# Attention and a rational MLP on one core: the local scores of a batch's first four heads in one burst on TensorE

## The chip, the cores and the metric

The kernel runs on one core of a Trainium2 chip. A core has TensorE (PE, with its weight loads shown apart as PEld), VectorE (DVE), ScalarE (ACT), GpSimd (POOL) and SyncE (SP); each works through its own list of instructions in order and waits on semaphores for the others. SP and POOL also issue DMA transfers. The time is device microseconds (us) of one execution, as the median of three runs.

## The reference

The input is q, k and v of 8 batches, 8 heads, 576 rows and 64 columns, and the weights and six coefficients of an MLP. All is float32.

```
q_d, k_d, v_d = mean over 4 neighbouring rows of q, k, v       # 144 rows
pooled = softmax(q_d k_d^T / 8) v_d, each row repeated 4 times
local  = softmax(q k^T / 8 where |i - j| < 4, else -1e9) v     # a band
x = (pooled + local), heads side by side                        # 4608 x 512
h = x @ w_in                                                    # 4608 x 2048
g = (a0 + a1 h + a2 h^2 + a3 h^3) / (1 + |b0||h| + |b1| h^2 + 1e-6)
out = g @ w_out                                                 # 4608 x 512
```

## The kernel before

**MLP.** Most of TensorE's time goes to the two products. A step takes a block of tokens through one piece of the 2048 columns. `h_part` multiplies into one of two PSUM banks, 2 and 3, which the steps use in turn: in fp32 from the decoded weights `wb` for the first 16 steps (L1546, four matmuls a step), and later from `xs` with the weights split in two fp32r parts `wh` and `wl` (L1560). ACT reads the bank four times with polynomials of h (`act`, L1574, into `m`, `n`, `gb`, `line`), DVE combines them (`rational`, L1603 to L1619, into `g` or `gg`), and `o_part` (L1639) multiplies with the second weights into banks 4 to 7. A bank of h can be written again when its four readers on ACT are done. In the first fifth of the run ACT and DVE also decode and split the weights (`sl` L573, `wb` L579, `wh` L596, `wl` L598).

**Attention.** It runs beside this, a batch ahead, with banks 0 and 1 for its scores. A `Half` is four heads of a batch in two pairs (`self.cs`). The band is computed on ten windows of 58 keys. For a half TensorE has three bursts of small matmuls between the big ones: `scores` (L999, 20 matmuls: the local scores of the first pair), `scores_rest` (L1041 and L1052, 32 matmuls: the local scores of the second pair and the pooled scores of both) and `weight_both` (L884 and L1372, 52 matmuls: the weighting with v). A batch has six such bursts from batch 3 on. What doesn't fit in banks 0 and 1 is lent from the two h banks for a moment (`Loan`): the next step that would use that bank waits for the DVE mask that empties it (L1082). DVE adds the mask to each pair's scores as it takes them from PSUM (L1009, L1082, L1091), then takes the row maximum (L1111), and ACT the exponentials (L1122). To turn the weights round, DVE transposes in blocks and SP sends the blocks out and back: four DMA issues `fd<-fx` for each pair (L1272), four `fp<-epb` for each half's pooled part (L1299).

In the small matmuls, two row tiles (the upper and lower 64 partitions) may write one bank. Where they do, `passed` and `behind` let PE signal SP and SP signal back, so that the second waits for the first. In `scores_rest` eight small matmuls stand between the two lines, and in `weight_both` many more; `scores` has no such hop.

```
                before = passed(local(3, 0))
...
                behind(local(0, 1), before)
```

**Order.** A `Plan` writes every engine's list before the kernel is built. Pieces are added with an engine, an estimated duration, what they read and write, and a due time; the plan lays them out by due times, pushes pieces that came late, and tries this 400 times from a fixed seed. Due times come from the constants at the file's end (`H_FIRST` and `H_STEP` for the MLP steps, `SCORES_EARLY`, `DUES`, `LEADS` for the bursts of a half, `KEEPDUE`, `FETCH`, `AHEAD`, `LATE` for weights, loads and so on). So one change in a piece or a constant moves pieces all over the program.

Of the kernel before, what the change touches and what calls it, by code (L numbers as in the profile page):

```python
# [15 lines left out]
ALU = mybir.AluOpType  # L16
# [5 lines left out]
P = 128  # L22
# [14 lines left out]
NW = 10  # L37
# [58 lines left out]
    )  # L96


class Plan:


# [70 lines left out]
    def run(self):  # L172


        kept = [(t, dict(t.preds), list(t.succs), t.lag) for t in self.tasks]

        def again():
            for t, preds, succs, lag in kept:
                t.preds, t.succs, t.lag, t.start = dict(preds), list(succs), lag, None
            return self.once()  # L180

        dice = random.Random(SEED)
        best, bias = None, [0.0] * len(kept)
        for n in range(PASSES):
            for t, x in zip(self.tasks, bias):
                t.bias = x
            if n:
                self.push(dice)
            tried = [t.bias for t in self.tasks]
            again()  # L190
# [30 lines left out]
    def once(self):  # L221
# [21 lines left out]
        while len(done) < len(self.tasks):  # L243
# [44 lines left out]
            if t.loan is not None:  # L288
                t.loan.room = self.turns[n][0]
                users = [x for x in t.succs if x.engine != "PE"]  # L290
                users = [x for x in users if t.loan.keys & x.takes]
                self.lent.setdefault(n, []).extend(users)
                if n + 2 in self.turns:
                    h = self.turns[n + 2][1][0]
                    for q in (open_["PE"], waiting["PE"]):
                        if any(x[2] is h for x in q):
                            q[:] = [x for x in q if x[2] is not h]
                            heapq.heapify(q)
                    todo = []
                    for x in users:  # L300
                        h.preds[x] = False
                        x.succs.append(h)
                        left[h] += 1
                        todo.append((x, h))
                    while todo:
                        x, y = todo.pop()
                        late = y.late - x.dur - self.gap(x, y)
# [19 lines left out]
def attention_moe(  # L327
# [631 lines left out]
    class Half:  # L959
# [64 lines left out]
                )  # L1024
            self.softmax(c)

        def scores_rest(self, bk):

            o = self.cs[1]
            n4 = NQ * SD  # L1030
            bc = Loan()

# [26 lines left out]
            def issue():  # L1059
# [14 lines left out]
                local(4, 0)  # L1074

            add(
                "PE", SREST, issue, (o.slot.qk, *(c.means for c in self.cs)), (*bk, bc),
                due=self.due - self.lead - SCORES_EARLY[1]
            ).step = ROOM[0]
            def masked():  # L1080
                n4_ = 4 * QD
                nc.vector.tensor_tensor(  # L1082
                    out=o.slot.eq.ap.rearrange("p b (j c) k -> p j b (c k)", j=2)[:, ::-1, :, :n4_],
                    in0=bc.ap.rearrange("p (j b n) -> p j b n", j=2, b=2),
                    in1=maskd.ap.rearrange("p b c k -> p b (c k)")[:, :, :n4_].unsqueeze(1).broadcast_to([P, 2, 2, n4_]),
                    op=ALU.add,
# [2 lines left out]
            def masked_last(g):  # L1089
                gs = slice(g * D, (g + 1) * D)  # L1090
                nc.vector.tensor_tensor(  # L1091
                    out=o.slot.eq.ap.rearrange("p b (j c) k -> p j c b k", j=2)[gs, :: 2 * g - 1, 4],
                    in0=two(bk)[gs, :, n4 : n4 + D].rearrange("p j (b k) -> p j b k", b=2),
                    in1=maskd.ap[gs, :, 4].unsqueeze(1).broadcast_to([D, 2, 2, QD]), op=ALU.add
                )
# [662 lines left out]
    for w, f, spot in chunks[len(early) :]:  # L1758
        weights(w, f, spot)

    def attend(b):

        if b == PFLIP:
            own = pools[0]
            pads = own.eb.ap.rearrange("p h b i k c -> p (h b i k) c")[:, :, QB:]
            add("POOL", 0.5, lambda: nc.gpsimd.memset(pads, 0.0), (), (own.e, *own.rooms))
        early, gap = (SPLIT_EARLY, QUAD_GAP) if b < LATER else ENDS
        last = due_h(blocks[b].first) - early - 3.0
# [38 lines left out]

    begun = []

    def begin_half(b, q):  # L1810
        early, gap = (SPLIT_EARLY, QUAD_GAP) if b < LATER else ENDS
        last = due_h(blocks[b].first) - early - 3.0
        bk = banks[0:2]
        k = 2 * (b - LATER) + q
        half_ = Half(b, q, last - (1 - q) * gap + (DUES[k] if k >= 0 else 0.0))
        half_.lead = LEADS[k] if k >= 0 else 0.0
        half_.load()
        c = half_.cs[0]
        if b in PEMASK:
            scores(c, bk)  # L1820
# [82 lines left out]
PAIRS = (14, 128)  # L1903
KEPT = 2
UNIT0 = 0
KEEPDUE = 307.365
FETCH = -15.499
O_LAG = 4.049
H0 = 20.57
H_FIRST = 5.91  # L1910
H_STEP = 5.979
SPLIT_EARLY = 5.529
QUAD_GAP = 42.0
LATER = 2
ENDS = (11.53, 52.06)
SCORES_EARLY = (38.82, 49.09)
WARM = 0.6
EP_DVE = (1, 3)
LEAD = 13.84
# [2 lines left out]
BOTH = 1  # L1922
SOON = 1.2
SPOTS = (0, 1, 2, 3, 6, 0, 1, 4, 5, 2, 3)
LATE = 0.083
MINUS = (0, 1, 2, 3)
POOLED = (2, 3)
VBANK = (0, 0)
POOLDUE = 0.0
FILL = 17  # L1930
KEEP = 3
AHEAD = 14.6
# [8 lines left out]
DUES = (-5.76, -9.77, -3.13, -7.81, -2.8, -4.74, -2.31, -2.62, -4.58, -8.38, -2.54, -4.74)  # L1941
LEADS = (0.17, 10.7, 5.25, -3.78, -8.15, -0.78, 0.3, -0.47, 2.8, 3.6, -2.67, -0.87)
AHEAD_S = 1
FLIPLAG = (3.4, 5.0, 4.5, 6.5)
FLIPSP = 2.0
# [80 lines left out]
```

## Time and profile before

| what | value |
|---|---|
| median of 3 runs | 919.04 us (918.35 to 919.2) |
| the profiled execution, its own time | 918.93 us |
| span of its records | 917.2 us |
| PE busy | 905.3 us, 99% |
| DVE busy | 836.4 us, 91% |
| ACT busy | 749.0 us, 82% |
| granted TensorE clock, mean | 0.999 |

The profiled execution is 0.11 us below the median, and 1.73 us of it lie around the span. PE has almost no idle time, but a busy PE isn't the same as a PE at its pace: records of matmuls overlap, so the pace is read from the distance between starts (a 128x512 matmul's record lasts 0.39 us, and the next one starts 0.23 us after it). Each float32 matmul on small tiles leaves two records, so a burst of 20 matmuls shows as x40.

### The profile page before, as it was taken

To read this page: it belongs to the slowest core of one execution; us is meant where nothing else is said; L and a number is where in the kernel's file an instruction comes from. 1 tells how busy PE (TensorE), PEld (TensorE's weight loads), DVE (VectorE), ACT (ScalarE), POOL (GpSimd) and SP (SyncE) were. 2 spreads that over 40 slices of the span, in tenths; PEclk is the share of its full clock that TensorE was granted. 3 is DMA by queue.
4 is the path that set the end of the run, shared out by engine and by line. 5 is a ranking of instruction groups with operands and counts; after the bars stand their busy time and mean duration, and the time that the engine had idled before them with its cause. 6 is when DMAs were issued, how large, how long until landed. Compare 5 with 4: busy or idle time off the path is not lost.

```text
span 917.2 us, 18534 instructions
## 1 busy us (share of the span) xinstructions
PE 905.3 (99%) x7039; PEld 718.6 (78%) x7039; DVE 836.4 (91%) x1004; ACT 749.0 (82%) x1738; POOL 171.9 (19%) x237
## 2 busy tenths in 40 slices
PE   8999999999999999999999999999999999999998
PEld 6655667888888888888888888888888888888886
DVE  8899999999998999989998999999899888788984
ACT  5899999978887879788897888787979776677853
POOL 3222022122311213031403131222210100110010
PEclk9999999999999999999999999999999999999999
DMA  9988888758894869687878778586944340224033
GB/s 317 333 241 254 254 218 233 205 127 216 185 302 129 210 181 215 222 176 223 200 248 182 243 181 264 141 248 183 262 121 132 134 137 1 92 92 138 1 115 114
DMA packets 85370, 171.28 MB, mean 187 GB/s; under 512 B 10914, under 2 KB 50338, under 8 KB 85282
## 3 DMA queue, kind: packets, MB, share of 16 engines
q0 software_dynamic: 32224, 72.30, 33.8%
q1 hardware_dynamic: 52914, 97.68, 31.7%
q8 instruction: 55, 0.90, 0.4%
q14 instruction: 33, 0.27, 0.1%
q10 hardware_dynamic: 144, 0.13, 0.1%
HBM read 140.58 MB, written 29.49 MB: 185 GB/s over the span
## 4 chain that ended last, share of the span: by engine, by line
PE 90%; ACT 7%; DVE 2%; issue 1%; DMA 1%; SPq 0%; DVEq 0%
PE psum L1639 41%; PE psum L1560 38%; PE psum L1546 3%; ACT m L1574 2%; PE psum L884 2%; ACT gb L1574 1%; PE psum L1372 1%; ACT el L775 1%; PE psum L1041 1%; PE psum L999 1%; PE psum L1052 1%; DMA qk<-in_qk_dram 1%; ACT wh L596 1%; ACT epc L806 1%; ACT sl L573 0%
## 5 line engine op out<-in xcount | busy, mean ns | idle before, releaser
L1639 PE MATMUL psum<-wh,gg 128*128 128x512 f32 x912 | 297.4, 393 | 0.0
L1560 PE MATMUL psum<-xs,wh 128*128 128x512 f32 x1024 | 256.4, 390 | 0.0
L1560 PEld LDWEIGHTS psum<-xs,wh 128*128 128x128 f32 x1024 | 191.3, 188 | 41.4 <-ACT n L1574 1.3
L1639 PEld LDWEIGHTS psum<-wh,gg 128*128 128x128 f32 x912 | 169.3, 188 | 36.2 <-DVE gg L1619 0.2
L1639 PE MATMUL psum<-wl,gg 128*128 128x512 f32 x456 | 177.6, 389 | 0.0
L1574 ACT ACTIVATE m<-psum,cf 128x512 f32<-128x512 f32 x172 | 128.4, 755 | 40.8 <-PE psum L1560 35.0
L1560 PE MATMUL psum<-xs,wl 128*128 128x512 f32 x512 | 137.1, 390 | 0.0
L1574 ACT ACTIVATE n<-psum,cf 128x512 f32<-128x512 f32 x116 | 86.3, 752 | 53.6 <-PE psum L1560 48.9
L1560 PEld LDWEIGHTS psum<-xs,wl 128*128 128x128 f32 x512 | 96.0, 188 | 20.0
L1639 PEld LDWEIGHTS psum<-wl,gg 128*128 128x128 f32 x456 | 85.6, 188 | 17.8
L1574 ACT ACTIVATE line<-psum,cf 128x512 f32<-128x512 f32 x114 | 91.1, 800 | 0.4 <-DVE m L1607 0.4
L656 POOL DMA_DIRECT2D vpc<-in_vp_dram x42 | 36.6, 872 | 242.8 <-DMA vpc<-in_vp_dram 231.6
L443 POOL DMA_DIRECT2D wl<-ws x48 | 31.3, 651 | 263.0 <-PE psum L1639 259.6
L1603 DVE SCALAR_TENSOR_TENSOR m<-m,cf,m 128x512 f32<-128x512 f32 (+1 forms) x58 | 58.1, 1002 | 18.2 <-ACT m L1574 18.0
L656 POOL DMA_DIRECT2D pqb<-in_qkb_dram x60 | 56.8, 995 | 81.2 <-DMA pqb<-in_qkb_dram 72.1
L1122 ACT ACTIVATE eq<-eq,nmb 128x64 f32<-128x64 f32 x200 | 66.8, 343 | 2.4 <-DVE nmb L1116 2.4
L1546 PE MATMUL psum<-xf,wb 128*128 128x512 f32 x128 | 59.6, 602 | 2.5 <-ACT gb L1574 1.6
L1639 PE MATMUL psum<-wh,g 128*128 128x512 f32 x160 | 56.8, 420 | 0.6 <-DVE g L1619 0.6
L1618 DVE TENSOR_TENSOR m<-m,m 128x512 f32<-128x512 f32 (+1 forms) x58 | 54.8, 945 | 1.0
L1606 DVE TENSOR_TENSOR m<-m,m 128x512 f32<-128x512 f32 (+1 forms) x58 | 54.5, 940 | 0.1
L1574 ACT ACTIVATE m<-psum 128x512 f32<-128x512 f32 x86 | 53.5, 623 | 0.5 <-PE psum L1560 0.5
L1603 DVE SCALAR_TENSOR_TENSOR n<-n,cf,n 128x1024 f32<-128x1024 f32 x29 | 37.1, 1279 | 13.3 <-ACT n L1574 13.2
(152 smaller groups left out, 1637.6 us busy)
## 6 DMA issues: line engine op xcount, KB each, us to landing
wh<-ws POOLq DMA_DIRECT2D x48, 512.0 KB, 5.4
wl<-ws POOLq DMA_DIRECT2D x48, 512.0 KB, 4.5
qk<-in_qk_dram SPq DMA_DIRECT2D x32, 590.0 KB, 6.3
vw<-in_vw_dram SPq DMA_DIRECT2D x32, 320.0 KB, 4.3
pqb<-in_qkb_dram POOLq DMA_DIRECT2D x60, 168.0 KB, 5.0
out_dram<-lv SPq DMA_DIRECT2D x32, 256.0 KB, 6.3
fd<-fx SPq DMA_DIRECT2D x96, 80.0 KB, 3.8
ef<-fd SPq DMA_DIRECT2D x24, 320.0 KB, 4.6
```

The lines of the kernel that those rows point to most:

```text
L443: "POOL", 1.0, lambda d=scratch[i][j], x=x: nc.gpsimd.dma_start(out=x.ap.bitcast(F32), in_=d),
L596: add("ACT", 0.88, lambda: nc.scalar.copy(out=hi.ap, in_=exact), (lo,), (hi,), due=due)
L656: lambda d=dst, x=x: nc.gpsimd.dma_start(out=d.ap, in_=x, accum_op=ALU.add),
L884: mms.append(nc.tensor.matmul(x.ap[j * D : (j + 1) * D, o : o + D].rearrange("p (a q) -> p a q", a=2), lhsT=c.slot.vw.ap[m : m + D, w, :], ...
L1122: nc.scalar.activation(out=e[:, n], in_=e[:, n], func=AF.Exp, bias=nm[:, n : n + 1], scale=scale, accum_out=sm[:, n : n + 1],)
L1546: nc.tensor.matmul(ph.ap, lhsT=bits2[0][fc // 2].ap[:, fc % 2, c, :].bitcast(F32), rhs=x.ap[:, c, :], start=(c == 0), stop=(c == NCC - 1),)
L1560: nc.tensor.matmul(ph.ap[:, f * t : (f + 1) * t], lhsT=(high, low)[j][0][fc].ap[:, c, :], rhs=blk.x[i].ap[:, c, :] if blk.b is not None el ...
L1574: return add("ACT", cost, lambda: nc.scalar.activation(out=to, in_=in_, func=func, **kw), (room_in, cf, *more), (out_,))
L1603: lambda: v.scalar_tensor_tensor(out=tb_, in0=tq_, scalar=b1, in1=tb_, op0=ALU.mult, op1=ALU.add),
L1606: dve(0.61, lambda: v.tensor_tensor(out=ta_, in0=ta_, in1=tq_, op=ALU.mult), (ta, tq), (ta,))
L1618: dve(0.61, lambda: v.tensor_tensor(out=tb_, in0=ta_, in1=tb_, op=ALU.subtract), (ta, tb), (tb,))
L1639: nc.tensor.matmul(ob[sub].ap, lhsT=g[i].ap[:, f0 : f0 + P], rhs=weight_out(k, fc, j).ap, start=(fc == 0 and m == 0), stop=(fc == NFC - 1 ...
```

## The change

From batch 3 on (`LENT[0]` is 3 before and after) a batch is written by a new function `attend_five`. The first half's `scores` gives way to `scores_two`, which issues the local scores of both pairs of that half, 40 matmuls, as one piece: 4 of the second pair's, then 20 of the first pair's, then 16 of the second pair's, the last 4 of them behind a hop over SP. Its output lies in banks 0 and 1 and in one lent bank, and three masks on DVE take it out. `scores_rest` then has the pooled scores of its own half and the local scores of one pair of the second half: the first half's call takes the second half's first pair, the second half's call its second pair. So a batch has bursts of 40, 32, 52, 32 and 52 matmuls, where it had 20, 32, 52, 20, 32 and 52. `weight_both` isn't changed. Beside this, many of the plan's constants have new values, and the plan goes on when a push leads it into a circle (`Stuck`).

```
+        def scores_two(self, bk):
+            a, o = self.cs
+            bc = Loan()
+            na, nb = NW // 2 * D, 3 * D
...
+            def issue():
+                mms = [one(o, k, j, j) for k in (3, 4) for j in range(2)]
+                before = passed(mms[2:])
+                for k in range(5):
+                    for j in range(2):
+                        for g in range(2):
+                            one(a, k, j, g)
+                for k in range(3):
+                    for j in range(2):
+                        for g in range(2):
+                            one(o, k, j, g)
+                behind([one(o, k, j, 1 - j) for k in (3, 4) for j in range(2)][:2], before)
+
+            add(
+                "PE", STWO, issue, (a.slot.qk, o.slot.qk), (*bk, bc, a.slot.el, o.slot.el), due=self.due - self.lead - SCORES_EARLY[0]
+            ).step = ROOM[0]
...
+            mask(a, lambda: both(0, na), 0, 5, bk, 0.74, 5)
+            mask(o, lambda: both(na, na + nb), 0, 3, bk, 0.47, 3)
+            mask(
+                o, lambda: bc.ap[:, : 4 * D].rearrange("p (j b n) -> p j b n", j=2, b=2), 3, 5, (bc,), 0.34, 2
+            )
+            self.softmax(a)
+            self.softmax(o)
+
+        def scores_rest(self, bk, o=None):
 
-            o = self.cs[1]
+            o = o or self.cs[1]
...
+    def attend_five(b):
+        bk = banks[0:2]
+        first = begun.pop()
+        first.load_rest()
+        second = make_half(b, 1)
+        second.load_one(0)
+        halves = first, second
+        for q, half_ in enumerate(halves):
+            invert(slots[0].sm, NW)
+            normalize(half_.cs[0], "local")
+            half_.flip(half_.cs[0])
+            if q:
+                half_.load_rest()
+            half_.scores_rest(bk, halves[1].cs[q])
+            half_.pooled(bk)
+            if q == 0:
+                second.load_one(1)
+                second.load_means()
+            elif b + 1 < B:
+                begun.append(begin_half(b + 1, 0))
+            half_.weight_both(bk)
+            if q and begun:
+                begun[0].load_rest()
...
+        if b >= LENT[0]:
+            half_.scores_two(bk)
+            return half_
...
-H_FIRST = 5.91
-H_STEP = 5.979
+H_FIRST = 5.786
+H_STEP = 5.967
...
-SCORES_EARLY = (38.82, 49.09)
+SCORES_EARLY = (-9.36, 48.83)
...
-SREST, ABOTH = 1.7, 2.2
-ROOM = (-0.63, 2.29, -4.75)
+SREST, ABOTH, STWO = 1.7, 2.2, 1.55
+ROOM = (-21.83, -2.37, -3.51)
...
```

Three places show what the new order is. The first is PE at the scores of a later batch's first heads; `qk0` and `qk1` are the loaded queries and keys of the two pairs, `xs` with `wh0`/`wl0` an h product, `gg` with `wh1`/`wl1` an o product. Before:

```order
L1560 MATMUL psum<-xs0_0_104,wl0_10_66 128x512 x4
L1639 MATMUL psum<-wh1_14_103,gg3_133 128x512 x4
L999 MATMUL psum<-qk0_156 64x2x32 x20
L1560 MATMUL psum<-xs0_0_104,wh0_12_94 128x512 x4
L1560 MATMUL psum<-xs0_1_105,wh0_12_94 128x512 x4
L1639 MATMUL psum<-wh1_12_102,gg0_130 128x512
```

After (L1724 is `o_part`, L1061 the merged burst):

```order
L1724 MATMUL psum<-wh1_14_103,gg2_132 128x512
L1724 MATMUL psum<-wl1_14_86,gg2_132 128x512
L1724 MATMUL psum<-wh1_14_103,gg3_133 128x512 x4
L1061 MATMUL psum<-qk1_162 64x2x32 x4
L1061 MATMUL psum<-qk0_156 64x2x32 x20
L1061 MATMUL psum<-qk1_162 64x2x32 x16
L1724 MATMUL psum<-wh1_12_102,gg0_130 128x512
```

The 20 matmuls have become 40 in one place between big matmuls, and an o product, not an h product, now follows them.

The second place is ACT at about 72 to 77 us, in the first fifth of the run; `m`, `gb` are the readers of an h bank, `et` and `eptc` copies for attention, `sl3` a weight's scales. Before:

```order
L596 CAST wh1_4_98<-wb1_4_77 128x1024
L1574 ACTIVATE m0_116<-psum,cf_146 128x512
L1574 ACTIVATE gb0_126<-psum,cf_146 128x512
L1574 ACTIVATE m1_117<-psum,cf_146 128x512
L1574 ACTIVATE m2_118<-psum 128x512
L848 ACTIVATE epc0_153<-epc0_153,smb0_150 128x3x48 x6
L1232 COPY et0_160<-psum 128x4x122
L1232 COPY et1_167<-psum 128x4x122
L1574 ACTIVATE m0_116<-psum,cf_146 128x512
L1574 ACTIVATE m1_117<-psum,cf_146 128x512
L1574 ACTIVATE m2_118<-psum 128x512
L1574 ACTIVATE gb2_128<-m1_117,cf_146 128x512
```

Next in that list stand `sl3`, a copy `eptc`, and then the fourth reader, `gb1<-psum`. After, from the same `gb0` on (L1659 is `act`):

```order
L1659 ACTIVATE gb0_126<-psum,cf_146 128x512
L1659 ACTIVATE m1_117<-psum,cf_146 128x512
L1659 ACTIVATE m2_118<-psum 128x512
L1659 ACTIVATE m0_116<-psum,cf_146 128x512
L860 ACTIVATE epc0_153<-epc0_153,smb0_150 128x3x48 x6
L1659 ACTIVATE gb1_127<-psum,cf_146 128x512
L1659 ACTIVATE m1_117<-psum,cf_146 128x512
L1659 ACTIVATE m2_118<-psum 128x512
L1659 ACTIVATE gb2_128<-m1_117,cf_146 128x512
L1317 COPY et0_160<-psum 128x4x122
L1317 COPY et1_167<-psum 128x4x122
```

The cast, both `et` copies, `gb2<-m1`, `sl3` and a copy `eptc` have moved from before the step's last reader of its h bank to behind it.

The third place is PE at the same time, around the product that waits for that bank. Before:

```order
L1546 MATMUL psum<-xf0_1_107,wb0_6_63 128x512 x4
L1190 MATMUL psum<-ident_141,epc0_153 112x112 x8
L1639 MATMUL psum<-wh1_2_97,g1_123 128x512
L1639 MATMUL psum<-wl1_2_74,g1_123 128x512
L1639 MATMUL psum<-wh1_2_97,g3_125 128x512 x4
L1546 MATMUL psum<-xf0_1_107,wb0_6_63 128x512 x2
```

After (L1631 is the fp32 h product, L1269 and L1275 transposes):

```order
L1631 MATMUL psum<-xf0_1_107,wb0_6_63 128x512 x3
L1269 MATMUL psum<-ident_141,el0_159 128x122 x4
L1269 MATMUL psum<-ident_141,el1_166 128x122 x4
L1631 MATMUL psum<-xf0_1_107,wb0_6_63 128x512 x3
L1275 MATMUL psum<-ident_141,epc0_153 112x112 x8
L1631 MATMUL psum<-xf0_1_107,wb0_6_63 128x512 x2
L1724 MATMUL psum<-wh1_2_97,g3_125 128x512 x4
```

The four o matmuls with `g3` and the eight transposes of `epc` stood ahead of the waiting product's matmuls and now stand among or behind them.

## Rows read from the trace of the kernel before

**Rows 1.** The page's head, and busy time by engine.
```profile
span 917.2 us, 18534 instructions
PE 905.3 (99%) x7039; PEld 718.6 (78%) x7039; DVE 836.4 (91%) x1004; ACT 749.0 (82%) x1738; POOL 171.9 (19%) x237
```

**Rows 2.** Waits of PE: what waited, for whom; us in total, times, longest.
```profile
PE psum L1546 <- ACT gb L1574: 1.6, 2, 1.3
```

**Rows 3.** Windows: us, busy (x count) by engine, PEclk, DMA share, GB/s.
```profile
60.00:80.00 20.00, 18.11 (x71) 11.03 (x69) 19.54 (x31) 19.97 (x46) 5.44 (x6) 1.00 0.89 272
300.00:500.00 200.00, 200.00 (x1628) 164.45 (x1628) 187.61 (x212) 169.45 (x428) 47.34 (x64) 1.00 0.78 207
```

**Rows 4.** Timeline of PE at a burst: start, duration, what; last, that line's group.
```profile
360.83 1.98 PE L1560 MATMUL psum<-xs,wh 128*128 128x512 f32 x8
362.65 1.07 PE L1560 MATMUL psum<-xs,wl 128*128 128x512 f32 x4
363.64 0.81 PE L999 MATMUL psum<-qk 64*64 64x64 f32 x40
364.39 2.12 PE L1560 MATMUL psum<-xs,wh 128*128 128x512 f32 x8
...
L999 PE MATMUL psum<-qk 64*64 64x64 f32 x400 | 8.1, 223 | 0.0
```

**Rows 5.** Timeline of PE where it waits; in brackets the idle time and its releaser.
```profile
65.88 0.39 PE L1639 MATMUL psum<-wl,g 128*128 128x512 f32 x1
66.86 1.39 PE L1639 MATMUL psum<-wh,g 128*128 128x512 f32 x5 [0.59 <-DVE g L1619]
...
73.56 0.93 PE L1190 MATMUL psum<-ident,epc 112*112 112x112 f32 x8
...
74.80 1.09 PE L1639 MATMUL psum<-wh,g 128*128 128x512 f32 x4
77.19 1.55 PE L1546 MATMUL psum<-xf,wb 128*128 128x512 f32 x3 [1.30 <-ACT gb L1574]
...
101.34 3.70 PE L1546 MATMUL psum<-xf,wb 128*128 128x512 f32 x8 [0.32 <-ACT gb L1574]
```

**Rows 6.** Timeline of ACT ahead of the wait at 77.19 us.
```profile
66.53 1.03 ACT L596 CAST wh<-wb 128x1024 fp32r<-128x1024 f32 x1
...
71.69 1.02 ACT L1232 COPY et<-psum 128x488 f32<-128x488 f32 x2
...
74.31 0.76 ACT L1574 ACTIVATE gb<-m,cf 128x512 f32<-128x512 f32 x1
74.92 1.18 ACT L573 ACTIVATE sl<-sl 128x1024 f32<-128x1024 f32 x1
75.96 0.50 ACT L1232 COPY eptc<-psum 112x384 f32<-112x384 f32 x1
76.32 0.83 ACT L1574 ACTIVATE gb<-psum,cf 128x512 f32<-128x512 f32 x1
```

**Rows 7.** Groups of DVE by shape: busy us, mean ns, idle before.
```profile
L1603 DVE SCALAR_TENSOR_TENSOR n<-n,cf,n 128x1024 f32<-128x1024 f32 x29 | 37.1, 1279 | 13.3 <-ACT n L1574 13.2
L1009 DVE TENSOR_TENSOR eq<-psum,maskd 128x640 f32<-128x640 f32 x10 | 8.2, 815 | 0.7 <-PE psum L999 0.7
L1082 DVE TENSOR_TENSOR eq<-psum,maskd 128x512 f32<-128x512 f32 x10 | 6.9, 686 | 1.6 <-PE psum L1041 1.6
```

**Rows 8.** Timelines of DVE and PE after a `scores_rest` burst.
```profile
486.44 0.69 DVE L1082 TENSOR_TENSOR eq<-psum,maskd 128x512 f32<-128x512 f32 x1 [1.26 <-PE psum L1041]
...
487.72 1.98 PE L1560 MATMUL psum<-xs,wh 128*128 128x512 f32 x8
```

**Rows 9.** SP by line: ns min/median/max, first and last start.
```profile
L1299 SPq DMA_DIRECT2D fp<-epb x40: 303/460/1289, 258.9 to 706.0; - x40
L1272 SPq DMA_DIRECT2D fd<-fx x96: 303/448/2245, 148.8 to 708.8; - x96
L946 SPq EVENT_SEMAPHORE  x22: 17/17/17, 180.7 to 725.6; - x22
```

More of the change, by code (lines that the diff above doesn't have):

```diff
@@ L96 @@
     )
+class Stuck(Exception):
+    pass
 class Plan:
@@ L189, in run @@
             tried = [t.bias for t in self.tasks]
-            again()
+            try:
+                again()
+            except Stuck:
+                for t, x in zip(self.tasks, bias):
+                    t.bias = x
+                again()
+                continue
             cost = max(t.end for t in self.tasks if t.engine == "PE")
@@ L1025, in scores, with load_one, load_means, one @@
             self.softmax(c)
-        def scores_rest(self, bk):
-            o = self.cs[1]
+        def load_one(self, i):
+            load_qk(self.cs[i])
+        def load_means(self):
+            load_pooled(self.cs, False)
+        def scores_two(self, bk):
+            a, o = self.cs
+            bc = Loan()
+            na, nb = NW // 2 * D, 3 * D
+            def one(c, k, j, g):
+                js = slice(j * D, (j + 1) * D)
+                w = (2 * k + g) * WQ
+                rows = slice(g * D, (g + 1) * D)
+                if c is a:
+                    to = bk[j].ap[rows, :na].rearrange("p (b c k) -> p b c k", b=2, k=QD)[:, :, k]
+                elif k < 3:
+                    to = bk[j].ap[rows, na : na + nb].rearrange("p (b c k) -> p b c k", b=2, k=QD)[:, :, k]
+                else:
+                    to = bc.ap[rows, : 4 * D].rearrange("p (j b c k) -> p j b c k", j=2, b=2, k=QD)[:, j, :, k - 3]
+                return nc.tensor.matmul(
+                    to,
+                    lhsT=c.slot.qk.ap[js, 0, PADL + w : PADL + w + D],
+                    rhs=c.slot.qk.ap[js, 1, w : w + D].rearrange("p (b k) -> p b k", b=2),
+                    start=True, stop=True, skip_group_check=True,
+                )
[14 more added lines that the diff above has]
+            ).step = ROOM[0]
+            def mask(c, src, lo, hi, rooms, cost, n):
+                add(
+                    "DVE", cost,
+                    lambda: nc.vector.tensor_tensor(
+                        out=c.slot.eq.ap.rearrange("p b (j c) k -> p j b c k", j=2)[:, :: 1 - 2 * c.odd, :, lo:hi].rearrange(
+                            "p j b c k -> p j b (c k)"
+                        ),
+                        in0=src(),
+                        in1=maskd.ap.rearrange("p b c k -> p b (c k)")[:, :, lo * QD : hi * QD].unsqueeze(1).broadcast_to(
+                            [P, 2, 2, (hi - lo) * QD]
+                        ),
+                        op=ALU.add,
+                    ),
+                    (*rooms, maskd), (c.slot.el,), lag=0.5,
+                )
+            def both(lo, hi):
+                return two(bk)[:, :, lo:hi].rearrange("p j (b n) -> p j b n", b=2)
+            mask(a, lambda: both(0, na), 0, 5, bk, 0.74, 5)
+            mask(o, lambda: both(na, na + nb), 0, 3, bk, 0.47, 3)
+            mask(
+                o, lambda: bc.ap[:, : 4 * D].rearrange("p (j b n) -> p j b n", j=2, b=2), 3, 5, (bc,), 0.34, 2
+            )
+            self.softmax(a)
+            self.softmax(o)
@@ L1076, in scores_rest @@
             add(
-                "PE", SREST, issue, (o.slot.qk, *(c.means for c in self.cs)), (*bk, bc),
+                "PE", SREST, issue, (o.slot.qk, *(c.means for c in self.cs)), (*bk, bc, o.slot.el),
                 due=self.due - self.lead - SCORES_EARLY[1]
@@ L1082, in masked @@
                 nc.vector.tensor_tensor(
-                    out=o.slot.eq.ap.rearrange("p b (j c) k -> p j b (c k)", j=2)[:, ::-1, :, :n4_],
+                    out=o.slot.eq.ap.rearrange("p b (j c) k -> p j b (c k)", j=2)[:, :: 1 - 2 * o.odd, :, :n4_],
                     in0=bc.ap.rearrange("p (j b n) -> p j b n", j=2, b=2),
@@ L1766, in attend @@
             add("POOL", 0.5, lambda: nc.gpsimd.memset(pads, 0.0), (), (own.e, *own.rooms))
-        early, gap = (SPLIT_EARLY, QUAD_GAP) if b < LATER else ENDS
-        last = due_h(blocks[b].first) - early - 3.0
+        if b >= LENT[0]:
+            attend_five(b)
+            return
         bk = banks[0:2]
@@ L1808, in attention_moe, with make_half @@
     begun = []
-    def begin_half(b, q):
+    def make_half(b, q):
         early, gap = (SPLIT_EARLY, QUAD_GAP) if b < LATER else ENDS
         last = due_h(blocks[b].first) - early - 3.0
-        bk = banks[0:2]
         k = 2 * (b - LATER) + q
@@ L1816, in begin_half @@
         half_.lead = LEADS[k] if k >= 0 else 0.0
+        return half_
+    def begin_half(b, q):
+        bk = banks[0:2]
+        half_ = make_half(b, q)
         half_.load()
+        if b >= LENT[0]:
+            half_.scores_two(bk)
+            return half_
         c = half_.cs[0]
@@ L1931 @@
 KEEP = 3
-AHEAD = 14.6
+AHEAD = -5.102
 RAMP = 10
```

20 lines of the change are left out of this document (11 added, 9 removed).

## The prediction

> **What bounds the kernel now.** I read the page's busy times first. PE is busy 905.3 of 917.2 us [rows 1], so the end is set by how closely PE's matmuls stand. The waits of PE come next: beyond the start-up the longest entry that repeats is a wait of the fp32 h product for ACT, 1.6 us in two waits, the longer 1.3 [rows 2]. It is small, but it says that in some stage PE isn't the bound. The windows show which. From 300 to 500 us PE is busy 200.00 of 200 us while DVE and ACT have 6% and 15% of their time free; from 60 to 80 us PE is busy 18.11 of 20, DVE 19.54 and ACT 19.97 [rows 3]. So there are two stages, and the change is priced in each by other means. In the late one any microsecond taken from PE's list is a microsecond of the end. In the early one PE waits for ACT and DVE, which have no free time, so what counts is the order in which these two do their work, and not what PE has to do.
>
> The burst of small matmuls has its price from the timeline around one [rows 4]. Eight big matmuls take 362.65 - 360.83 = 1.82 us, 0.2275 each. The four that start at 362.65 would have their successor at 363.56; it starts at 364.39, 0.83 us later, and the eight from there take 2.12 us instead of 1.98, 0.14 more. A burst of 20 small matmuls so costs 0.97 us.
>
> **The change part by part.**
>
> *The merge.* A batch's small matmuls are as many as before: 40 + 32 + 52 + 32 + 52 = 208, and twice 20 + 32 + 52 is 208. What falls is the number of times that PE goes from big to small and back: five bursts instead of six, in five batches (3 to 7), so five in all. Of the 0.97 us a part grows with the matmuls. The burst's 40 records last 0.81 us from first start to last end; one lasts 0.223 us in the mean, so 0.81 - 0.22 = 0.59 us lies over 39 distances, 0.015 each, and 40 of them are 0.61 us [rows 4]. What is left, 0.97 - 0.61 = 0.36 us, goes with the burst and not with its size. Five fewer: 5 x 0.36 = 1.8 us less. Nothing hides this, since PE doesn't wait in that stage [rows 3]. From both sides: if the fixed part came from neighbours that now merely stand elsewhere, the gain is 0; if all 0.97 us went, it would be 4.9, which the unchanged matmuls exclude. I take 1.8.
>
> *The masks and the rest of the merged burst's work.* DVE took two pairs' scores with masks of 640 columns (0.815 us) or of 512 and smaller [rows 7], and now takes 640, 384 and 256. From 0.815 at 640 and 0.686 at 512 a column costs 0.0010 us, so 384 and 256 cost 0.56 and 0.43 by that slope. The work on DVE stays about the same, and in the late stage DVE has 6% free to hide a difference of some tenths. I cost it at 0; the wait it can bring is a term below.
>
> *The order of the first fifth.* This has nothing to do with merging: the merged bursts begin at batch 3, but the new due times move pieces from the start of the run. Three waits of PE stand there with rows. The time lost by one is the distance between two starts less 0.227: at 66.86 us 66.86 - 65.88 - 0.23 = 0.75 us (the profile calls 0.59 of it idle, so 0.16 of a loss isn't shown as idle). At 77.19 the last start before is 74.80 + 3 x 0.227 = 75.48, so 1.71 - 0.23 = 1.48 us. At 101.34 it is 0.32 + 0.16 = 0.48 us. Together 2.71 us [rows 5].
>
> The one at 77.19 can be followed step by step. The product waits for ACT's last reader of its h bank, the `gb` at 76.32 us [rows 6]. Before that reader ACT does five kinds of work that the new order puts behind it: the cast (1.03), the two `et` copies (1.02), the other `gb` (0.76), the scales (1.18) and a copy `eptc` (0.50). That is 4.49 us by duration; consecutive records overlap by about 0.14 (74.31 + 0.76 - 74.92 is 0.15), five times 0.14 is 0.7, so the reader comes 3.8 us earlier. But PE comes earlier too: four o matmuls (0.91) and the eight transposes, which with two o matmuls fill the time from 73.56 to 74.80 (1.24 - 0.45 = 0.79), no longer stand ahead of it, and the loss at 66.86 is gone by my count, 0.75 more. So the gate opens 3.8 us earlier, PE arrives 2.45 earlier, and of a wait of 1.48 only 1.48 - 1.35 = 0.13 is left. At 66.86 the product waits for DVE's `g`; two decodings of weights stood ahead of it on DVE and now stand behind. At 101.34 four instructions of ACT have left the place ahead of the last reader, two of them casts like the one at 66.53, for 0.4 us by which PE is earlier. I take both losses as gone. This term is 2.71 - 0.13, so 2.6 us less. Its bounds are 0, if the moved work is itself late, and 2.71. I take a value near the upper end because ACT, 0.03 us idle in 20, does the same work in any order and only its order is at stake [rows 3]. What is late next is what was moved: the casts, on which o products wait. That is the first rival.
>
> *New waits.* A merged burst has a hop over SP where `scores` had none. PE waits there for SP's nop, and behind it on PE stand the last 4 small matmuls and all that follows; on SP the nop stands behind whatever SP issues. The 22 hops of before took SP 17 ns each [rows 9], and PE lost nothing that shows in the middle of the run [rows 3]. In the new list on SP, three of the five merged bursts' hops stand right behind the four issues `fp<-epb`, and three of ten `scores_rest` bursts have the four issues `fd<-fx` just ahead of their hop. Four issues take 4 x 0.460 = 1.84 us or 4 x 0.448 = 1.79 at the median [rows 9]. The cover of a merged burst is 36 matmuls, 72 records of 0.015: 1.09 us. So a hop costs nothing if the set of issues has begun 0.75 us or more ahead of the burst, and at most 0.75 at the median if it begins with it.
>
> The Trainium skill, TensorEngine Tiling (Array Packing), section Restrictions and Gotchas, says that row tiles can't access the same PSUM bank at once and that software must keep them apart. That speaks against a merge, since it is why the new burst needs a hop; the trace agrees only so far that 22 such hops are there and cost nothing that shows. By the rule alone a hop is necessary, and its price is still that of SP's queue.
>
> The merged burst also lends an h bank: PE's next product into it waits for the last of three masks, 0.82 + 0.56 + 0.43 = 1.8 us after the burst, and up to 1.28 more if DVE has just begun a combining operation [rows 7]. In the new list 11 to 20 matmuls (2.5 to 4.5 us) stand between. After `scores_rest` it is 6 to 10 matmuls against 0.69 and up to 1.28. The nearest row for that is at 486 us: the mask ends at 487.13, the product starts at 487.72, with 0.59 us to spare [rows 8]. For all these new waits I take 0.5 us, about one set of issues late with little cover, from 0 to the sums of the second and third rivals (there is no gain in them, as a wait can't give time back).
>
> *The sum.* 918.93 - 1.8 - 2.6 + 0.5 = 915.0 for the profiled execution; it lies 0.11 below the median, so 915.1 us.
>
> **The rivals.**
>
> *Only the merge counts.* The waits of the first fifth come back, because the casts that were moved behind the readers now come late for the o products, or DVE's moved decodings do. For it: ACT and DVE have no free time there, so what they do later they do late for someone. Against it: a cast is fetched ahead, and the `wh` cast at 66.53 served a later step than the one running. The time: 919.04 - 1.8 + 0.2, for a small new wait, so 917.4.
>
> *Slower: SP comes late at the hops.* If SP begins its set of issues only when the burst begins, a merged burst loses 0.75 us and a `scores_rest` burst, whose hop has 8 matmuls of cover, up to 1.79. Three of each: 2.3 + 5.4 = 7.6, on top of 915.1 - 0.5 = 914.6: 922.2 us. It decides from (920.9 - 914.6) / 6 = 1.05 us per burst. For it: a single issue has taken 1.29 and 2.25 us [rows 9]. Against it: SP's issues are released by DVE's transposes, and only an unlucky moment puts them within a microsecond of the burst.
>
> *The lent banks come back late.* At the closest places, covers of 11 to 13 matmuls after merged bursts and of 6 or 7 after `scores_rest`, the worst case of 1.28 us in flight loses 0.1 to 0.6 us each; eight places come to at most 3.6: 914.6 + 3.6 = 918.2. Against it: DVE waited 1.26 us for the burst at 486 us [rows 8], so it is often idle when the mask is due.
>
> *The merge saves nothing*, since what I call the fixed part belongs to the first small matmuls of each kind. Then 915.1 + 1.8 = 916.9.
>
> **How the numbers follow.** The forecast, 915.1, has 0.64; only the merge 0.14; SP late 0.12; lent banks late 0.05; the merge saves nothing 0.05. The forecast's own range goes from 914.2 (no new wait, and 0.4 of other neighbours in the first fifth) to 916.2. The range for 8 in 10 reaches on to the first rival: 914.2 to 917.9. What a measurement here can tell from no change is about 0.2%, 1.84 us: faster is below 917.2, slower above 920.9. Faster are the forecast (0.64), the merge without a gain (0.05), and of the first rival and SP late in one burst or two 0.05 together: 0.74. Slower is SP late at five bursts or more: 0.08. The rest, 0.18, is within.
>
> **What would show it.** In the profile after, the waits of PE for ACT between 60 and 125 us are gone or under 0.3 us; a burst of 40 matmuls, worked out as above, costs about 0.97 + 0.61 = 1.58 us there are five of them, and no burst of 20 is left; the masks of 384 and 256 columns take about 0.56 and 0.43 us. The prediction is wrong if PE has new waits for `wh` or `wl` in the first fifth, if a merged burst lasts much over 1.5 us (that is SP's hop), or if a big matmul waits for a mask behind a burst.

## The result: slower by 1%

The changed kernel takes 928.51 us (median of 4 runs, 926.09 to 928.67) against 919.12 (918.35 to 919.9) beside it: a ratio of 1.0095 (95% interval 1.0084 to 1.0107), and 9.4 us between the two medians. Forecast were 915.1 us and a range up to 917.9. The page's head after:

```profile
span 926.7 us, 18517 instructions
PE 909.3 (98%) x7039; PEld 720.6 (78%) x7039; DVE 838.0 (90%) x1009; ACT 746.6 (81%) x1738; POOL 172.0 (19%) x237
```

The span is 9.5 us longer [rows 1], and the number of matmuls and of ACT's instructions is the same. PE's busy time is only 4 us longer, so most of the loss is waiting. The longest waits of PE after (us in total, times, longest) that before didn't have, or had elsewhere (it waited 0.6 us for `g` at 66.86 us [rows 5]):

```profile
PE psum L1126 <- SPq L958: 1.9, 1, 1.9
PE psum L1645 <- ACT line L1659: 1.7, 3, 0.9
PE psum L1645 <- ACT n L1659: 1.4, 1, 1.4
PE psum L1724 <- DVE gg L1695: 1.1, 1, 1.1
PE psum L1724 <- DVE g L1695: 0.8, 1, 0.8
```

The wait for `gb` [rows 2] is gone, as forecast; but the fp32r products (L1645) and the o products (L1724) now wait for ACT and DVE in the stage where before PE never waited. The windows show where (the two of [rows 3], then 60 to 125 us; columns as there):

```profile
60.00:80.00 20.00, 20.00 (x96) 12.75 (x96) 19.68 (x31) 20.00 (x44) 3.76 (x5) 1.00 0.97 318
300.00:500.00 200.00, 197.99 (x1618) 162.96 (x1617) 184.23 (x209) 165.94 (x423) 47.41 (x63) 1.00 0.76 206
60.00:125.00 65.00, 64.70 (x448) 40.46 (x447) 64.68 (x100) 64.50 (x160) 12.52 (x15) 1.00 0.87 249
```

From 60 to 80 us PE is busy all the time, where it missed 1.9 us. From 300 to 500 us it misses 2.0 us, where it missed none. Idle time understates a loss, as in the prediction, so the losses are taken here from distances between starts:

| where | us |
|---|---|
| four waits in the late stage, at 366, 466, 564 and 666 us: 1.27 + 1.06 + 1.53 + 0.78, and 0.11 each in the matmul behind | +5.1 |
| one late hop at 638 us (the burst's 64 records start over 3.58 us, not 1.33) | +2.25 |
| eight big matmuls at half clock behind that hop | +1.5 |
| a wait for `g` at 833 us | +1.1 |
| five merged bursts for ten of 20 | -1.1 |
| what is left, up to some 180 us | +0.6 |
| sum | +9.5 |

**A merged burst** in PE's timeline:

```profile
412.77 1.07 PE L1724 MATMUL psum<-wh,gg 128*128 128x512 f32 x4
413.77 1.55 PE L1061 MATMUL psum<-qk 64*64 64x64 f32 x80
415.26 0.50 PE L1724 MATMUL psum<-wh,gg 128*128 128x512 f32 x1
415.59 0.40 PE L1724 MATMUL psum<-wl,gg 128*128 128x512 f32 x1
```

The last big matmul would have had its successor at 412.77 + 4 x 0.2275 = 413.68; it comes at 415.26, 1.58 us later, and the first one behind takes 0.33 us to its successor, 0.10 more. The burst costs 1.68 us, with the 0.14 of [rows 4] for the end 1.72, and two bursts of 20 cost 1.94. So a merge saves 0.22 us, not 0.36. All five are alike, and none waits at its hop.

**A wait of the late stage.** PE's timeline at 466 us, and ACT's ahead of it:

```profile
464.50 0.39 PE L1724 MATMUL psum<-wl,gg 128*128 128x512 f32 x1
465.79 1.43 PE L1645 MATMUL psum<-xs,wh 128*128 128x512 f32 x5 [0.90 <-ACT line L1659]
```

```profile
460.38 1.98 ACT L860 ACTIVATE epb<-epb,smb 128x144 f32<-128x144 f32 x6
462.23 1.09 ACT L1770 COPY lv<-psum 128x512 f32<-128x512 f32 x2
463.17 0.65 ACT L1659 ACTIVATE n<-psum 128x512 f32<-128x512 f32 x1
463.66 1.41 ACT L1659 ACTIVATE n<-psum,cf 128x512 f32<-128x512 f32 x2
464.89 0.84 ACT L1659 ACTIVATE line<-psum,cf 128x512 f32<-128x512 f32 x1
```

PE wants an h bank whose fourth reader is `line` at 464.89. ACT has waited for nothing since 455.3 us: six scalings of pooled weights, two output copies, and only then the four readers. The waits at 366, 564 and 666 us have a like picture, with the six `epb` scalings ahead of the last two readers, at 666 with four `lv` copies behind them (or, at 366, with both ahead of the `m` that DVE's `gg` needs).

**The late hop.** SP's timeline (the set of four issues, then its last one alone), PE's, and the window of PE behind it:

```profile
634.77 3.38 SPq L1357 DMA_DIRECT2D fd<-fx  x4
636.11 2.05 SPq L1357 DMA_DIRECT2D fd<-fx  x1
```

```profile
636.04 0.29 PE L1137 MATMUL psum<-pqb 64*64 64x144 f32 x2
638.27 0.27 PE L1126 MATMUL psum<-qk 64*64 64x64 f32 x2 [1.94 <-SPq L958]
...
638.88 2.27 PE L1724 MATMUL psum<-wh,gg 128*128 128x512 f32 x5
```

```profile
638.90:642.60 3.70, 3.70 (x11) 2.92 (x10) 3.54 (x6) 0.00 (x0) 1.44 (x2) 0.54 0.50 115
```

This is a `scores_rest` burst, not a merged one. SP began four issues 0.4 us ahead of the burst and took 3.38 us for them (four at the median would be 1.8 [rows 9]), 2.05 of it for the last one alone; the hop stood behind. The big matmuls after it ran at a granted clock of 0.54, about the lower of the two levels (1.2 GHz), 0.427 us apart instead of 0.2275.

### The profile page after: what moved, and what is told of

It reads as the page before. It is cut to its first block, busy times and chain, and to the rows that moved or that the text cites. A ratio compares the mean times of both kernels' runs of the same rounds, so it can differ in the third digit from the quotient of the medians.

```text
span 926.7 us, 18517 instructions
## 1 busy us (share of the span) xinstructions
PE 909.3 (98%) x7039; PEld 720.6 (78%) x7039; DVE 838.0 (90%) x1009; ACT 746.6 (81%) x1738; POOL 172.0 (19%) x237
## 4 chain that ended last, share of the span: by engine, by line
PE 74%; ACT 11%; DVE 10%; issue 2%; DMA 1%; SPq 0%; DVEq 0%; ACTq 0%
PE psum L1724 34%; PE psum L1645 33%; ACT m L1659 3%; PE psum L896 2%; PE psum L1457 1%; ACT lv L1770 1%; ACT epb L818 1%; DVE wb L591 1%; PE psum L1126 1%; ACT epb L860 1%; PE psum L1631 1%; PE psum L1061 1%; ACT gb L1659 1%; ACT eq L1207 1%; PE psum L1137 1%
## 5 line engine op out<-in xcount | busy, mean ns | idle before, releaser
L1724 PE MATMUL psum<-wh,gg 128*128 128x512 f32 x912 | 301.9, 395 | 2.0 <-DVE gg L1695 1.1
L1645 PE MATMUL psum<-xs,wh 128*128 128x512 f32 x1024 | 257.0, 391 | 3.2 <-ACT line L1659 1.7
L1645 PEld LDWEIGHTS psum<-xs,wh 128*128 128x128 f32 x1024 | 191.7, 188 | 45.6 <-ACT line L1659 3.2
L1724 PEld LDWEIGHTS psum<-wh,gg 128*128 128x128 f32 x912 | 170.7, 188 | 40.1 <-DVE gg L1695 1.5
L1724 PE MATMUL psum<-wl,gg 128*128 128x512 f32 x456 | 178.2, 391 | 0.0
L1659 ACT ACTIVATE m<-psum,cf 128x512 f32<-128x512 f32 x172 | 127.3, 747 | 39.0 <-PE psum L1645 38.5
L1645 PE MATMUL psum<-xs,wl 128*128 128x512 f32 x512 | 137.0, 389 | 0.0
L1659 ACT ACTIVATE n<-psum,cf 128x512 f32<-128x512 f32 x116 | 85.5, 749 | 35.1 <-PE psum L1645 35.1
L1645 PEld LDWEIGHTS psum<-xs,wl 128*128 128x128 f32 x512 | 96.0, 188 | 20.0
L1724 PEld LDWEIGHTS psum<-wl,gg 128*128 128x128 f32 x456 | 85.9, 188 | 17.5
L1659 ACT ACTIVATE line<-psum,cf 128x512 f32<-128x512 f32 x114 | 89.7, 789 | 0.7 <-DVE m L1692 0.7
L668 POOL DMA_DIRECT2D pqb<-in_qkb_dram x60 | 54.8, 997 | 77.4 <-DMA pqb<-in_qkb_dram 72.9
L1207 ACT ACTIVATE eq<-eq,nmb 128x64 f32<-128x64 f32 x200 | 67.0, 347 | 0.0
L1631 PE MATMUL psum<-xf,wb 128*128 128x512 f32 x128 | 59.8, 604 | 1.0 <-DVE xf L924 0.8
L1659 ACT ACTIVATE lg<-n,cf 128x1024 f32<-128x1024 f32 x29 | 33.7, 1162 | 31.1 <-DVE n L1688 30.9
L1724 PE MATMUL psum<-wh,g 128*128 128x512 f32 x160 | 57.5, 422 | 0.1
L1659 ACT ACTIVATE m<-psum 128x512 f32<-128x512 f32 x86 | 53.0, 616 | 4.4 <-PE psum L1645 4.4
```

The costliest lines, as they stand in the source:

```text
L668: lambda d=dst, x=x: nc.gpsimd.dma_start(out=d.ap, in_=x, accum_op=ALU.add),
L1207: nc.scalar.activation(out=e[:, n], in_=e[:, n], func=AF.Exp, bias=nm[:, n : n + 1], scale=scale, accum_out=sm[:, n : n + 1],)
L1631: nc.tensor.matmul(ph.ap, lhsT=bits2[0][fc // 2].ap[:, fc % 2, c, :].bitcast(F32), rhs=x.ap[:, c, :], start=(c == 0), stop=(c == NCC - 1),)
L1645: nc.tensor.matmul(ph.ap[:, f * t : (f + 1) * t], lhsT=(high, low)[j][0][fc].ap[:, c, :], rhs=blk.x[i].ap[:, c, :] if blk.b is not None el ...
L1659: return add("ACT", cost, lambda: nc.scalar.activation(out=to, in_=in_, func=func, **kw), (room_in, cf, *more), (out_,))
L1724: nc.tensor.matmul(ob[sub].ap, lhsT=g[i].ap[:, f0 : f0 + P], rhs=weight_out(k, fc, j).ap, start=(fc == 0 and m == 0), stop=(fc == NFC - 1 ...
```

## The experiments

The table gives each kernel's median and its ratio to the kernel before, run beside it. An A or B behind a time is the theory of the expectation that the run bears out.

| run | us | ratio, 95% interval |
|---|---|---|
| six_new_due | 920.25 | 1.0016 (1.0006 to 1.0025) |
| merge_old_due | 932.72 | 1.0156 (1.0141 to 1.0171) |
| hop_first | 924.99 | 1.0065 (1.0050 to 1.0080) |
| less_act | 923.94 | 1.0050 (1.0034 to 1.0067) |
| hop_less_act | 922.52 | 1.0030 (1.0020 to 1.0039) |
| merge_batch4 | 924.03 | 1.0043 (1.0030 to 1.0057) |
| tidy | 924.64 | 1.0061 (1.0040 to 1.0082) |
| merge_tuned | 926.74 | 1.0084 (1.0062 to 1.0106) |
| held_4 | 930.97 | 1.0123 (1.0100 to 1.0146) |
| six_ahead_old | 922.18 | 1.0035 (1.0023 to 1.0047) |

**Merge or due times?** Two runs take the change apart. The first keeps the six bursts under all the new constants:

```
-        if b >= LENT[0]:
+        if FIVE and b >= LENT[0]:
             attend_five(b)
...
+FIVE = False
```

> Six bursts a batch as before, but all of the new due times and constants; the first 120 us of the list are those of the changed kernel. Theory A (the merge itself brings the new waits, because with five bursts the list no longer fits ACT's work between the readers of the h banks): the four waits of PE for ACT and DVE at 366, 466, 564 and 666 us (4.6 us with their group's 0.11 each about 5.1) and the late hop at 635 us with its slow matmuls (3.9 us) are gone; time 917.5 to 920. Theory B (the retuned due times bring them): the time stays within 2 us of the changed kernel's 928.5.

920.25 us: A by the waits, and 0.25 us above its range in time. The four waits and the late hop aren't there; the wait near 833 us is (at 825 us), and there are two smaller ones, 0.7 us for an ACT reader at 155 us and 0.4 us at 525 us, where a weighting burst waits for its flipped weights. The second keeps the merge and takes back the constants that the change had set anew (from `KEEPDUE` to `LEADS`):

```
-SCORES_EARLY = (-9.36, 48.83)
+SCORES_EARLY = (38.82, 49.09)
...
```

> Five bursts a batch with the due times and constants of the kernel before. Theory A (the merge itself brings the waits; the new due times only soften them): slower than the changed kernel, 930 us or more, with waits of PE of 1 us and more between 240 and 700 us. Theory B (the retuned due times bring the waits): about 917 to 919, that is the time before less some 1 us for the merged bursts.

932.72 us: A again. Its longest waits:

```profile
PE psum L1645 <- ACT line L1659: 5.5, 3, 3.0
```

With the same constants the merge costs 8.3 us by the medians (928.51 against 920.25), with the old ones 13.7. The new due times are worth 4 us to the merged kernel and cost the unmerged one about 1.2.

**What the merge does to ACT.** Since six_new_due and the changed kernel have the same constants and stand within 3 us of each other up to 425 us, their windows can be laid side by side. First the changed kernel, then six_new_due; in each the exponentials of the local scores alone (L1207: ACT's busy time and records, two to an exponential), then all:

```profile
425.00:467.00 42.00, 10.47 (x60) 1.00 0.81 224
467.00:495.00 28.00, 0.00 (x0) 1.00 0.66 195
...
425.00:467.00 42.00, 41.10 (x332) 33.69 (x331) 40.20 (x50) 38.95 (x117) 12.37 (x17) 1.00 0.81 224
```

```profile
425.00:467.00 42.00, 7.08 (x40) 1.00 0.77 201
467.00:495.00 28.00, 4.14 (x25) 1.00 0.74 229
...
425.00:467.00 42.00, 42.00 (x373) 34.55 (x372) 38.83 (x46) 36.08 (x96) 12.36 (x17) 1.00 0.77 201
```

Ahead of the wait at 466 us the changed kernel has done 30 exponentials, those of three pairs; with six bursts ACT has done 20, and the third pair comes behind 467 us. That is 3.4 us more of one kind and 2.9 more in all, in a stretch that ends with PE idle for 0.9 us. The third pair is the second half's first: with six bursts it has a burst of its own at 460 us, with five it is scored in the first half's `scores_rest` at 439.55, 21 us earlier. The other waits have the same shift: in the changed kernel that pair's exponentials begin at 350.4, 448.6, 549.1 and 647.6 us, ahead of the waits at 366, 466, 564 and 666 us; in six_new_due they begin at 371.9, 480.3, 570.6 and 667.2. In batch 3 they also come earlier (251.1 and 278.9), and PE doesn't wait, so the shift alone isn't enough.

**Is it ACT's backlog?** The lists stay as they are, and ACT does 4 of 6 scalings less for a half:

```
-            for i in range(NQ):
+            for i in range(NQ if c.b < PFLIP else 1):
```

> The changed kernel with the same lists, but from batch 3 on ACT scales one of the three parts of a pair's pooled weights, not three (4 of 6 instructions, 1.3 us, are left out for a half; the output isn't the reference's). Theory A (ACT's backlog ahead of the readers makes PE wait): the waits at 466, 564 and 666 us shrink by up to 1.3 each and the one at 366 too; time 924 to 925. Theory B (ACT only follows another engine, DVE's chain or a transfer): less than 1 us changes.

923.94 us, 4.6 less than the changed kernel: A, within 0.1 us of its range. The waits there are now, of those for ACT's readers:

```profile
PE psum L1724 <- ACT line L1659: 0.2, 1, 0.2
PE psum L1645 <- ACT line L1659: 0.2, 1, 0.2
PE psum L1645 <- ACT n L1659: 0.2, 1, 0.2
```

The wait at 466 us is gone, the others cost 0.2 to 0.4 us, and a new one of 0.6 us, for DVE's `gg`, stands at 575 us. In the profiled execution the late hop, too, costs only 0.6 us and not 2.25, though its set again begins 0.4 us ahead of the burst (at 632.19 us):

```profile
631.81 1.77 SPq L1357 DMA_DIRECT2D fd<-fx  x4
```

The four issues took 1.77 us here and 3.38 there. So the size of that loss is in part the chance of one execution, and this run alone doesn't price the backlog.

**The hop.** In SP's list the sets that start up to 1.5 us ahead of a scores burst go behind its hop:

```
     todo = plan.run()
+    for t in [x for x in todo if x.engine == "PE" and x.step is not None and x.dur in (STWO, SREST)]:
+        for x in [y for y in todo if y.fn.__name__ == "leave" and t.start - 1.5 < y.start <= t.start]:
+            todo.remove(x)
+            todo.insert(todo.index(t) + 1, x)
```

> The changed kernel with one edit in the list of SP: where a set of four issues fd<-fx starts up to 1.5 us ahead of a scores burst, it is put behind the burst's hop. Theory A (the late hop costs the 2.0 us of PE's wait at 638 us and also the slow matmuls right after it, 1.6 us, since the clock fell in the wait): 924.6 to 925.2. Theory B (the clock would have fallen anyway): about 926.4. Theory C (SP is late for another reason, or the moved set makes the weights late): 928 or more.

924.99 us: A, the slow matmuls belong to the hop. The span fell by 4.0 us to 922.7. SP and PE at the same burst, whose big matmuls began at 638.88 us in the changed kernel:

```profile
635.73 2.90 SPq L1357 DMA_DIRECT2D fd<-fx  x4
```

```profile
636.33 1.43 PE L1724 MATMUL psum<-wh,gg 128*128 128x512 f32 x5
```

The set still takes 2.9 us, now beside the big matmuls, which are 0.2275 us apart again. Both edits at once:

> Both edits at once on the changed kernel: the sets of issues fd<-fx behind the hops, and one of the three parts of a pair's pooled weights scaled on ACT from batch 3 on (the other two are left out, so the output isn't the reference's). Theory A (the loss has two parts that add: the late hop, and ACT's backlog ahead of the readers; what is left are a wait at the end of about 1.1 us, 0.5 us of the first fifth, and 1.0 us gained by the merge): 919.5 to 921, with no wait of PE of more than 0.4 us between 200 and 700 us. Theory B (with these gone the next waits come in their place): 922 or more.

922.52 us: B, by the time and by a wait of 0.7 us that A excludes. In the profile (a span of 919.4 us, in an execution of 922.98) losses of 0.4, 0.3, 0.7 and 0.2 us are left at 365, 561, 575 and 661 us; the one at 575 us is less_act's. The two edits take 3.5 and 4.6 us alone and 6.0 together, so they don't add: some of less_act's share was the hop's. Beside hop_first, from which it differs in ACT's work alone, the run is 2.5 us faster by the medians; so much of the backlog this edit takes away.

**The merged burst's missing gain.** In the merged burst the first and last four matmuls run as pairs; here matmuls of the other pair fill them up to four:

```
-                mms = [one(o, k, j, j) for k in (3, 4) for j in range(2)]
+                mms = []
+                for k in (3, 4):
+                    mms += [one(o, k, j, j) for j in range(2)]
+                    for j in range(2):
+                        one(a, k - 3, j, 1 - j)
                 before = passed(mms[2:])
...
```

> The run hop_first with one edit: in the merged burst the first four and the last four matmuls, which ran two at a time, are mixed with matmuls of the first pair so that four run at a time, as in the rest of the burst. Theory A (the merged burst's missing gain, 1.0 us for five bursts and not 1.8, lies in these two ends, 0.13 us a burst): the burst's 80 records last 1.20 us from first to last start, not 1.34; the time is 0.65 us less than hop_first, 924.3. Theory B (it lies in the hop): unchanged, 925.0.

The burst in its timeline:

```profile
413.21 1.40 PE L1061 MATMUL psum<-qk 64*64 64x64 f32 x80
414.54 0.50 PE L1733 MATMUL psum<-wh,gg 128*128 128x512 f32 x1
```

1.33 us to the next big matmul, not 1.49, in all five: A for the place. The profiled span is 921.7 us, 1.0 less than hop_first's; the medians (924.64 and 924.99) are too wide apart in their runs to tell 0.8 us. With these ends a burst of 40 costs 1.56 us and a merge saves 0.38 us.

**One merge.** Six bursts and the new constants, but `FIVE = (4,)` with `b in FIVE`.

> Six bursts a batch and the new due times, as in the run six_new_due (920.25), but batch 4 alone has the merged burst. Theory A (a merge costs by itself, since both pairs' softmax then stand on ACT at once): slower than 920.25 by 1 to 2 us, 921.3 to 922.3, with a wait of PE for ACT or DVE in that batch. Theory B (one merge is harmless, and only five of them in a row leave no slack): 920.0, that is 0.2 less.

924.03 us, more than either theory gives. In batch 4 PE loses 0.7 us at 369.5 and 0.3 at 367 to waits for ACT and DVE: 1.0 us, as A has it. A hop at 490 us, in the next batch, loses 0.6. But this list also came out otherwise in the first 180 us, with some 2.4 us more of waits there, so the total says nothing on one merge.

**Can it be mended?** Two tries, both on tidy. Other due times:

> The run tidy with due times of the same constants searched again, for a list in which less work stands ahead of the readers of the h banks. Theory A (the waits of the merge can be softened by due times, but not taken away): two to four waits of PE for ACT or DVE between 360 and 660 us, of 0.4 to 0.9 us each; 921 to 923, slower than the kernel before. Theory B (a fit list makes the merge pay): 918 or less.

926.74 us: A for the waits, slower than either theory for the time. Its waits in the late stage are still there, and a weighting burst waits 1.0 us for its flipped weights:

```profile
PE psum L1654 <- ACT line L1668: 1.5, 2, 1.0
...
PE psum L896 <- DMA ef<-fd: 1.0, 1, 1.0
PE psum L1733 <- DVE gg L1704: 0.9, 1, 0.9
PE psum L1654 <- ACT n L1668: 0.8, 1, 0.8
```

And the early pair's exponentials held back by 4 us (`self.softmax(o, HELD if o not in self.cs else None)`, the value being the lag behind the row maximum's scaling):

> The run tidy, but the exponentials of the second half's first pair, which the merge brings onto ACT some 20 us earlier (with scores_rest of the first half, not with a burst of its own), may begin no sooner than 4 us after their row maximum. Theory A (they come too early, ahead of the readers of the h banks, and can simply be held back): the waits at 365, 465, 563 and 661 us shrink and the time is below 924. Theory B (they can't be held, since the pair's buffers are wanted again by the next merged burst, which needs the buffers of both pairs at once): more waits, 926 or more.

930.97 us: B. Its longest waits:

```profile
PE psum L1733 <- DVE gg L1704: 2.9, 1, 2.9
PE psum L1654 <- ACT line L1668: 2.3, 2, 1.3
```

So the pair can't simply be held. That its buffers are then late for the next merged burst, which needs those of both pairs at once, is the reason that the code suggests; the run shows only that holding costs more. PE also waits 1.0 us at a hop of `weight_both` (at 639 us), which the edit in SP's list leaves where it was.

**The wait at the end.**

> The run six_new_due (six bursts, all new constants) with one constant, AHEAD, of the kernel before; it sets how far ahead of their due time the h products of the last steps stand. Theory A (AHEAD brings the wait of PE for g near 825 us, which every list with the new constants has): no wait of more than 0.3 us there, and the last 100 us are 1.1 us shorter. Theory B (another constant does): the wait of 1.0 us stays.

B: PE loses 1.0 us to `g` at 827 us, as in six_new_due. The list with AHEAD alone put back also got another wait, a loss of 1.3 us at 465 us, so the time (922.18) says nothing on the constant's own cost:

```profile
PE psum L1645 <- ACT line L1659: 1.1, 1, 1.1
```

This is the wait of the late stage without a merge, so a new list can bring one by itself. What the merge brings is their number. Between 360 and 680 us, counting PE's idle times of over 0.5 us for ACT or DVE, the kernel before and six_new_due have none and six_ahead_old this one; the four different lists with five merges (the changed kernel, merge_old_due, merge_tuned, held_4) have three or four.

Which constant brings the wait near 830 us stays open; merge_old_due, with none of the new ones, doesn't have it.

None of these runs beats the kernel before, and none points to a list that would.

## Why the prediction was wrong

*What bounds the kernel.* Right for the moment of the trace, wrong as a rule. "In the late one any microsecond taken from PE's list is a microsecond of the end" holds only while the readers of the h banks stay ahead of PE. DVE and ACT had 6% and 15% free on the mean of 200 us [rows 3]; on ACT the free time lies in pieces. Two windows of the kernel before show it (columns as in [rows 3]; ACT is the fourth figure behind the length):

```profile
446.00:453.00 7.00, 7.00 (x32) 5.80 (x31) 6.90 (x8) 7.00 (x27) 3.28 (x5) 1.00 0.92 179
481.00:488.00 7.00, 7.00 (x89) 5.70 (x88) 5.63 (x8) 2.52 (x4) 1.76 (x2) 1.00 0.75 193
```

This is the step that failed: "the masks and the rest of the merged burst's work" was costed at 0 by the amount of work, which is indeed the same, and not by when it reaches ACT. It costs 5.1 us. That the merge brings these waits (six_new_due) and that ACT's work ahead of the readers makes them (less_act) is shown; that the pair 21 us early is what fills ACT is read from the windows, and no run isolates it. Looking at the PE list alone, I followed the merged burst, and not the pair that the merge passes on to `scores_rest` 21 us early.

The Trainium skill, TensorEngine Tiling (Array Packing), section Performance Considerations, says that tiling speeds up TensorE but not the evacuation of PSUM. The evacuation itself was no trouble here: the masks of 384 and 256 columns took 0.55 and 0.41 us, as worked out (columns as in [rows 7]). What didn't get faster with PE was the softmax behind it.

```profile
L1088 DVE TENSOR_TENSOR eq<-psum,maskd 128x384 f32<-128x384 f32 x5 | 2.8, 550 | 0.0
L1088 DVE TENSOR_TENSOR eq<-psum,maskd 128x256 f32<-128x256 f32 x5 | 2.1, 414 | 0.0
```

*The merge.* The mechanism is right, and the size is off: 0.22 us a burst and not 0.36, 1.1 us and not 1.8. A burst of 40 was forecast at 1.58 and costs 1.72, because its two ends run two matmuls at a time (tidy); with four at a time the forecast 0.36 us is there.

*The order of the first fifth.* The three waits went, as forecast, and the busy time from 60 to 80 us shows it. But the gain of 2.6 us was given back by 180 us, and 0.6 more: new waits of some tenths stand at 98, 120, 136, 155, 161 and 169 us. This is the first rival's case. Its reason, late casts, isn't what the waits name (ACT `line` at 136 us, for one); which work was late I didn't trace. The new due times bring it without the merge too: six_new_due waits 0.7 us at 155 us.

*New waits.* Taken at 0.5. The merged bursts' hops and the lent banks cost nothing, as the sum said. The one late hop was that of a `scores_rest` burst, from the group of three that the second rival names; one issue of 2.05 us, near the slowest of [rows 9], made its set 3.38 us long. With one burst of six late the rival is right in its place, not in its count, and its price was too low: 2.25 us against up to 1.79. That the clock falls behind such a wait and costs another 1.5 us was in no term. Most of the 3.75 us hangs on that one issue: with 1.77 us for the set the same hop lost 0.6 us (less_act).

*The end.* The sum has no term for the last 100 us; the new constants cost 1.1 us there, at 833 us (six_new_due has this wait too).

*The sum.* Against the forecast stand 5.1 us for the readers, 3.2 for the first fifth (0.6 lost, by what the table leaves, and not 2.6 gained), 3.25 for the hop and the clock (3.75 and not 0.5), 0.7 for the merge and 1.1 for the end: 13.4 us, from 915.1 to the 928.5 measured. Of the three signs of being wrong none came (no wait for `wh`, `wl` or a mask, and a merged burst lasts 1.55 us): none of them looks at the readers.

*The chances.* 0.08 on slower was too little: all rivals but one ended below the 919.04 of the kernel before, because each took its price from PE's list or from a wait right behind a burst. A rival "the readers come late" was to be had from ACT's windows above.

## What to carry to other kernels

Where one engine is never idle, its list can be shortened only as long as the engines that feed it keep their distance; price a merge by when its products reach the next engine, with that engine's busy time in windows as short as a buffer's turn, not by its share of the whole. A change of structure and a retuning of its constants should be run apart: here the one cost 13.7 us with the old constants and the other hid 4 of them. A hop through a queue that also issues transfers cost nothing that shows 26 times of 27 in the changed kernel and 3.8 us once, behind one slow issue; put the issue behind the hop.

## What the runs showed of the hardware

A wait of PE of 1.94 us was followed by eight matmuls at the lower granted clock, 0.427 us apart; waits of 3.0 us (merge_old_due) and 2.9 us (held_4) were too, and the other waits of these lists between 200 and 900 us, of 1.6 us (merge_old_due, at 566 us) and less, weren't. Here are merge_old_due's:

```profile
466.15 2.77 PE L1645 MATMUL psum<-xs,wh 128*128 128x512 f32 x8 [3.01 <-ACT line L1659]
468.72 1.91 PE L1645 MATMUL psum<-xs,wl 128*128 128x512 f32 x4
```

The first five behind the wait still start 0.23 to 0.34 us apart, and the slow ones follow. The Trainium skill, TensorE: Matmul & The Clock Gate, Part 1, gives 426.7 ns between starts for 512 columns at the lower level; the trace's 0.426 to 0.427 us agree.
